# Second mixture-of-experts layer on one core: weight operands stored in order of use, their splits spread over other steps, and stores, splits and sums moved where the layers meet

## The chip, the cores and the metric

One of the eight NeuronCores of a Trainium2 chip runs the program. The metric is device time in microseconds (us) from start to end of one execution. TensorE (PE) multiplies, VectorE (DVE) and ScalarE (ACT) copy, split and add, GpSimd (POOL) adds and issues DMAs, SyncE (SP) issues DMAs. Each engine takes its instructions in the order in which they are written and waits for others through semaphores.

## What is computed

```python
# 2304 tokens: q, k, v are (4, 8, 576, 64); all is fp32 (the first layer's weights come as float64)
kv  = einsum('bhsd,bhse->bhde', k, v)
out = einsum('bhsd,bhde->bhse', q, kv)
x   = out / sqrt(mean(out*out, -1) + 1e-6) * g_norm            # -> (2304, 512)
h   = maximum(maximum(x @ w1, x @ w2), x @ w3)                 # 768 wide
y   = h @ w_out                                                # (2304, 512)
p   = probs / (probs.sum(-1) + 1e-9)                           # 4 experts
for e in range(4):                                             # the second layer
    out += p[:, e:e+1] * (maximum(y @ e_w1[e], 0) @ e_w2[e])   # 1024 wide
```

## The kernel before

Attention and most of the first layer fill the trace up to about 360 us. The change concerns the second layer and the stretch in which it takes over from the first, which is called **the turn** here.

**Tiling of the second layer.** The tokens are six blocks of 384, two to a superblock (`sb` 0, 1, 2). The hidden units of the four experts are eight halves, the **passes** (`q` 0 to 7). A pass goes over the three superblocks, forwards or backwards in turn; a pass and a superblock make a **visit** (24 of them, `gi`). Both matrix products are done by a 2x2 block scheme with seven products in place of eight (Winograd's). Each fp32 operand is split into a high part in the PE's reduced format and a low part (what is left), and high x high, low x high and high x low are summed.

A visit has two **half-visits**, `n` = 0 to 47 (`r = n % 2`), and each of these has seven **steps**, `k` = 0 to 6. In a step the PE does `product(r, k)` of the first matrix product (six matmuls of 384 columns, line 605), then ACT and DVE take the sums out of two PSUM banks (`A` and `X`) in `after_product`, then the PE does 8 to 10 matmuls of 256 columns (line 866, `AFTER`) of the second matrix product of the visit before, whose results are scaled and stored by `after_second`. So the second product lags a visit behind. The last visit's second product stands alone at the end.

**Within a step.** The bank sequence of the seven products is A X A X A A X. After product 0 ACT copies A into X (line 659, `bank<-bank`) and product 1 adds to it, so product 1 waits for the copy. After product 4 ACT takes A out as `t22` and DVE adds X to it (line 646, `fa<-bank`), and product 6, which writes X, waits for that sum. After product 6 DVE adds X to `t12` (line 682), and the next half-visit's copy into X waits for it. What becomes the second product's operands is split later, by a table of steps (`later`, `todo`).

**Weights.** While half-visits 0 to 5 of a pass run, the next pass's weights come in: `w1_load` and `w2_load` (SP queue), the block sums of the scheme (`w1_sums` line 530, `w2_sums` line 559), and the splits: a high part by ACT (lines 536 and 565), then a low part by DVE (lines 500 and 566), 0.8 to 1.2 us each. Each operand has seven 256-column pieces; the split is done in two parts, of pieces 0 to 2 and 3 to 6. The second product uses its pieces in the order `j` = 0, 1, 3, 2, 5, 4, 6, and piece `j` stands in place `j`. A table, `plan`, filled by `at(n, step, function, ...)`, says after which step each of these is written; what is due runs at the end of its step.

**Activations.** A superblock's seven split operands (`y_split(k)`: ACT line 591, DVE line 500) are made in pass 0 from `y` (loaded from DRAM buffers `y_d` by `y_load`, with sums `y_sum`, line 582), stored to DRAM (`op_store`, line 1125) and loaded again in the later passes, one after each product that has freed its place (`op_load`, line 1129). A load into a place waits for those that still read it; an ACT or DVE write into a buffer waits for a DMA that still reads it.

**The turn.** Half-visits 0 and 1 have no earlier visit; half-visit 0 does the rest of the first layer's last product between its steps (`FILL_18`), half-visit 1 nothing. `y_put` (line 439) and `rest1` (line 791) store the first layer's last two blocks of results to `y_d` straight from buffers in the tile `fa`, which half-visit 1 uses again for `t12`, `t22` and their like.

Of the kernel before, what the change touches and what calls it, by code (L numbers as in the profile page):

```python
# [21 lines left out]
def tile_attn_moe_moe2(  # L22
# [28 lines left out]
    P = 128  # L51
# [381 lines left out]
    def y_put(j, c, bank, t):  # L433

        if c % 2 and j < 4:
            nc.vector.tensor_copy(out=t, in_=bank)
        else:
            nc.scalar.activation(out=t, in_=bank, func=AF.Copy)
        nc.sync.dma_start(out=y_rows(j, c), in_=t)
# [29 lines left out]
    SPLIT = {(8, 1): (0,), (8, 2): (1,), (8, 4): (2,), (8, 6): (3,), (0, 0): (4,), (0, 2): (5,), (0, 3): (6,)}  # L469
# [62 lines left out]
    def w1_split(r, half, early=False):  # L532
        cols = slice(0, 3 * 2 * P) if half == 0 else slice(3 * 2 * P, 7 * 2 * P)
        hi, lo = w1_slot(r)
        src = w1_at(early)[half][:, 2 * P if half == 0 else 0 :]
        nc.scalar.activation(out=hi[:, cols], in_=src, func=AF.Copy)  # L536
        low(lo[:, cols], src, hi[:, cols])

# [6 lines left out]
    def w2_load(q, r):  # L545
        e, pr = q // 2, q % 2 * 2 + r
        st = w2_at(q, r).rearrange("p (n d) -> p n d", n=8)
        for a, (x, y) in enumerate(((0, 7), (2, 4))):
# [102 lines left out]
    def after_product(n, k):  # L651
# [127 lines left out]
    def rest1(sb, p, blk, c):  # L779
# [10 lines left out]
        if p == NPF - 1:  # L790
            nc.sync.dma_start(out=y_rows(2 * sb + 1, c), in_=y)
# [5 lines left out]
    YLAG = 3  # L797
# [98 lines left out]
    with tc.manual_schedule():  # L896
# [354 lines left out]
```

## Time and profile before

| | us |
|---|---|
| median of 3 runs (lowest, highest) | 1131.92 (1130.12, 1133.57) |
| the profiled execution | 1131.67 |
| its span, first to last instruction | 1129.9 |
| PE busy (share of the span) | 1078.0 (95%) |
| DVE busy | 768.4 (68%) |
| ACT busy | 591.7 (52%) |

The span leaves out what lies around the first and the last instruction, 1.8 us here. An engine is busy while an instruction of it runs; in the matmul engine's case the ends are modelled, so that what counts is its idle time and what ended it. The half-visits of the second layer start at 360.5 us (n = 0), and the last step of the last one at 1103.5 us.

### The profile page before, as it was taken

The numbers are of one execution on the slowest core, as the hardware profiler recorded it, in microseconds if no ns is written. First come the engines' busy times: TensorE is split into PE (matmuls) and PEld (weight loads), VectorE is DVE, ScalarE is ACT, GpSimd is POOL, SyncE is SP. The second block draws the span as 40 slices with busy tenths as digits, with TensorE's granted clock in tenths as the row PEclk, the third lists the DMA queues.
The fourth block names the chain that finished last, engine by engine and source line by source line (L and its number), as shares of the span: only waits on it lengthen the run. The fifth ranks groups of instructions, "written<-read, shape, count | busy, mean of one in ns | idle before, by whom it ended". The sixth has DMA issues, their size and how long they took to land.

```text
span 1129.9 us, 19220 instructions
## 1 busy us (share of the span) xinstructions
PE 1078.0 (95%) x7318; PEld 1056.9 (94%) x7318; DVE 768.4 (68%) x1434; ACT 591.7 (52%) x1257; POOL 236.1 (21%) x261
## 2 busy tenths in 40 slices
PE   7889999999999799999999999999999999999997
PEld 6789999999998699999999999999999999999997
DVE  3789985667666877765765675675576577567545
ACT  2544224434343567555565565666556566556551
POOL 1346632430101001112111212112212211121111
PEclk8999999999999899999999999999999999999998
DMA  9955555431512858359577667768858957766875
GB/s 248 293 149 170 158 177 201 137 112 65 172 44 94 304 218 288 122 224 287 96 238 235 145 183 222 192 138 223 238 102 243 269 114 225 221 158 171 226 193 113
DMA packets 110460, 209.17 MB, mean 185 GB/s; under 512 B 13856, under 2 KB 68128, under 8 KB 110368
## 3 DMA queue, kind: packets, MB, share of 16 engines
q1 hardware_dynamic: 90704, 171.44, 45.8%
q0 software_dynamic: 18960, 36.19, 18.5%
q8 instruction: 57, 0.93, 0.3%
q10 hardware_dynamic: 704, 0.33, 0.1%
q14 instruction: 35, 0.29, 0.1%
HBM read 137.93 MB, written 69.99 MB: 184 GB/s over the span
## 4 chain that ended last, share of the span: by engine, by line
PE 59%; DVE 16%; DMA 8%; issue 7%; ACT 7%; SPq 1%; POOL 1%; DVEq 0%; ACTq 0%; POOLq 0%
PE bank L605 33%; PE bank L866 21%; PE bank L772 4%; DMA w_da<-cv_a 1%; PE bank L424 1%; DMA w1s<-in_moe_w_dram 1%; DMA y_d<-fa 1%; DMA out_dram<-ob 1%; DMA out_dram<-w2s 1%; DVE wr L566 1%; DVE wl L500 1%; ACT wl L536 1%; ACT ob L847 1%; DVE rb L500 1%; DVE cv_a L233 1%
## 5 line engine op out<-in xcount | busy, mean ns | idle before, releaser
L866 PE MATMUL bank<-wr 128*128 128x256 f32 x1701 | 263.6, 283 | 5.0 <-DVE wr L566 2.8
L866 PEld LDWEIGHTS bank<-wr 128*128 128x128 f32 x1701 | 239.5, 190 | 5.8 <-DVE wr L566 3.4
L605 PE MATMUL bank<-rb,wl 128*128 128x384 f32 x1032 | 210.4, 339 | 8.3 <-ACT bank L659 8.2
L659 ACT ACTIVATE fa<-bank 128x384 f32<-128x384 f32 x192 | 94.9, 494 | 179.2 <-PE bank L605 172.2
L605 PEld LDWEIGHTS bank<-rb,wl 128*128 128x128 f32 x1032 | 175.3, 188 | 11.5 <-ACT bank L659 10.3
L605 PE MATMUL bank<-xr,wl 128*128 128x384 f32 x864 | 176.3, 339 | 6.4 <-DVE fa L646 4.6
L605 PEld LDWEIGHTS bank<-xr,wl 128*128 128x128 f32 x864 | 145.9, 189 | 8.8 <-DVE fa L646 6.4
L641 DVE TENSOR_TENSOR wr<-fa,wr 128x384 fp32r<-128x384 f32 x131 | 72.3, 552 | 47.8 <-ACT wr L634 47.6
L866 PE MATMUL bank<-wr,hr 128*128 128x256 f32 x558 | 93.0, 285 | 1.7 <-DVE wr L566 1.7
L824 POOL DMA_DIRECT2D out_dram<-w2s x48 | 48.5, 1037 | 200.1 <-DVE ob L849 152.0
L824 POOL DMA_DIRECT2D out_dram<-ob x48 | 48.0, 1038 | 173.2 <-DVE w2s L849 93.2
L866 PEld LDWEIGHTS bank<-wr,hr 128*128 128x128 f32 x558 | 82.0, 192 | 2.1 <-DVE wr L566 2.1
L634 ACT ACTIVATE wr<-fa 128x384 fp32r<-128x384 f32 x152 | 78.4, 529 | 5.2 <-DVE fa L646 2.4
L866 PE MATMUL bank<-wr,xr 128*128 128x256 f32 x405 | 68.1, 281 | 0.9 <-DVE wr L566 0.9
L748 DVE TENSOR_TENSOR fa<-bank,fa 128x384 f32<-128x384 f32 x54 | 29.9, 554 | 51.6 <-ACT fa L745 36.3
L605 PE MATMUL bank<-op,wl 128*128 128x384 f32 x288 | 59.7, 343 | 5.2 <-ACT fa L659 5.2
L847 ACT ACTIVATE w2s<-bank,p_all 128x256 f32<-128x256 f32 x104 | 49.4, 475 | 24.6 <-PE bank L866 24.6
L847 ACT ACTIVATE ob<-bank,p_all 128x256 f32<-128x256 f32 x102 | 48.4, 474 | 24.9 <-PE bank L866 24.1
L824 POOL DMA_DIRECT2D out_dram<-fa x37 | 34.2, 1053 | 128.8 <-DVE fa L849 72.0
L866 PEld LDWEIGHTS bank<-wr,xr 128*128 128x128 f32 x405 | 59.1, 188 | 1.1 <-DVE wr L566 1.1
L530 POOL TENSOR_TENSOR w1s<-w1s 128x256 f32<-128x256 f32 x40 | 35.2, 898 | 110.2 <-DMA w1s<-in_moe_w_dram 48.9
L682 DVE TENSOR_TENSOR fa<-bank,fa 128x384 f32<-128x384 f32 x48 | 26.6, 554 | 43.6 <-PE bank L605 43.5
(204 smaller groups left out, 2037.3 us busy)
## 6 DMA issues: line engine op xcount, KB each, us to landing
rb<-op_d SPq DMA_DIRECT2D x42, 768.0 KB, 5.0
xr<-op_d SPq DMA_DIRECT2D x42, 768.0 KB, 6.5
out_dram<-w2s POOLq DMA_DIRECT2D x47, 256.0 KB, 6.4
out_dram<-ob POOLq DMA_DIRECT2D x46, 256.0 KB, 6.6
op<-op_d SPq DMA_DIRECT2D x14, 768.0 KB, 8.1
stage_a<-in_moe_w_dram SPq DMA_DIRECT2D x18, 512.0 KB, 4.1
w1s<-in_moe_w_dram SPq DMA_DIRECT2D x30, 256.0 KB, 3.8
out_dram<-fa POOLq DMA_DIRECT2D x30, 256.0 KB, 6.6
```

What stands on the lines that cost most here:

```text
L500: nc.vector.tensor_tensor(out=lo, in0=src, in1=f32(hi), op=ALU.subtract)
L530: eng.tensor_tensor(out=st[o], in0=st[a], in1=st[b], op=ALU.subtract)
L605: nc.tensor.matmul(out, w[wi][:, c * P : (c + 1) * P], y[yi][:, c, :], start=(i == 0 and k in begin), stop=(i == 5), skip_group_check=k no ...
L634: nc.scalar.activation(out=ops[key][0], in_=src, func=AF.Relu if relu else AF.Copy)
L641: nc.vector.tensor_tensor(out=lo, in0=src, in1=f32(hi), op=ALU.subtract)
L659: nc.scalar.activation(out=out, in_=in_, func=func)
L682: nc.vector.tensor_tensor(out=t12, in0=x, in1=t12, op=ALU.add)
L748: nc.vector.tensor_tensor(out=mx[done] if i == 0 else t, in0=x, in1=t, op=ALU.add)
L772: nc.tensor.matmul(bank[:, :T], w[:, wi, c * P : (c + 1) * P], h[a, blk][hi], start=((blk == 1 or p == 0) and a == 0 and n == 0), stop=((b ...
L824: nc.gpsimd.dma_start(out=rows, in_=src, accum_op=ALU.add)
L847: nc.scalar.activation(out=o, in_=piece(ps, i), func=AF.Copy, scale=pe)
L866: nc.tensor.matmul(piece(ps, i), h[hi][:, i * P : (i + 1) * P], w[wi], start=fresh, stop=last, skip_group_check=True,)
```

## The change

The second product's pieces stand in the order of use (`n` in place of `j`), and `w2_load` and `w2_sums` put the blocks where that order wants them. A split is now two functions, the high part (`w1_hi`, `w2_hi`) and the low part (`w1_lo`, `w2_lo`), and the table puts the low part one step behind the high part. Loads, sums and splits of the weights have other steps. The sum `t22` is written right behind ACT's part of step 4, and not after the second product's results of that step. At the turn, the last two blocks' stores go to POOL's queue, three `op_store` of superblock 0 come two or three steps later, `w1_load` of the next pass comes at n = 1, and the sums and splits of superblocks 1 and 2 come two steps later. At the end, the last operands' steps are written between the matmuls of the last second product, no longer all ahead of it, and the stores of each block's middle tile go to ACT's queue.

```diff
-        nc.sync.dma_start(out=y_rows(j, c), in_=t)
+        (nc.gpsimd if j == 4 else nc.sync).dma_start(out=y_rows(j, c), in_=t)
...
-    SPLIT = {(8, 1): (0,), (8, 2): (1,), (8, 4): (2,), (8, 6): (3,), (0, 0): (4,), (0, 2): (5,), (0, 3): (6,)}
+    SPLIT = {(8, 1): (0,), (8, 2): (1,), (8, 4): (2,), (0, 0): (3,), (0, 1): (4,), (0, 2): (5,), (0, 3): (6,)}
...
+    def w1_hi(r, half, early=False):
+        hi, lo, src = w1_cols(r, half, early)
+        nc.scalar.activation(out=hi, in_=src, func=AF.Copy)
+
+    def w1_lo(r, half, early=False):
+        hi, lo, src = w1_cols(r, half, early)
+        low(lo, src, hi)
...
-        for a, (x, y) in enumerate(((0, 7), (2, 4))):
+        for a, (x, y) in enumerate(((0, 7), (3, 5))):
...
+    def w2_hi(q, r, half):
+        hi, lo, src = w2_cols(q, r, half)
+        nc.scalar.activation(out=hi, in_=src, func=AF.Copy)
+
+    def w2_lo(q, r, half):
+        hi, lo, src = w2_cols(q, r, half)
+        nc.vector.tensor_tensor(out=lo, in0=src, in1=f32(hi), op=ALU.subtract)
...
-            later(t0 + 4, nc.vector.tensor_tensor, out=t22, in0=x, in1=t22, op=ALU.add)
+            nc.vector.tensor_tensor(out=t22, in0=x, in1=t22, op=ALU.add)
...
-            nc.sync.dma_start(out=y_rows(2 * sb + 1, c), in_=y)
+            (nc.gpsimd if sb == 2 else nc.sync).dma_start(out=y_rows(2 * sb + 1, c), in_=y)
...
-    YLAG = 3
+    YLAG = (0, 5, 5)
...
-                nc.sync.dma_start(out=rows, in_=src)
+                (nc.scalar if i == 1 else nc.sync).dma_start(out=rows, in_=src)
...
-        for j in (0, 1, 3, 2, 5, 4, 6):
+        for n, j in enumerate((0, 1, 3, 2, 5, 4, 6)):
...
-                    w = [t[:, j * 2 * P : (j + 1) * 2 * P] for t in w2_slot(r)]
+                    w = [t[:, n * 2 * P : (n + 1) * 2 * P] for t in w2_slot(r)]
...
-            at(0, 5 + i, w2_split, 0, 0, i)
+            at(*((0, 5), (1, 2))[i], w2_hi, 0, 0, i)
+            at(*((0, 6), (1, 3))[i], w2_lo, 0, 0, i)
+            at(*((1, 6), (2, 1))[i], w2_hi, 0, 1, i)
+            at(*((1, 6), (2, 2))[i], w2_lo, 0, 1, i)
...
-            at(0, (0, 1, 2, 3, 5, 5, 5)[k], op_store, 0, k)
...
+                at(2 * sb - 1, (4 + i, (1, 3, 5, 6)[i])[sb - 1], y_sum, nc.vector, i)
+        for k in range(7):
+            at(0, (0, 1, 2, 3, 7, 8, 8)[k], op_store, 0, k)
+            for sb in range(1, NSB):
+                at(2 * sb - 1, k + YLAG[sb], y_split, k)
+                at(2 * sb, k + 1, op_store, sb, k)
...
-            at(n - 2, 0, w1_load, e, pr)
-            at(n - 1, 5, w1_load, e, pr + 1)
+            at(n - 5, 2, w1_load, e, pr)
+            at(n - 1, 4, w1_load, e, pr + 1)
+            at(n, 1, w1_sums, nc.vector)
...
-                at(n - 2, 5 + i, w1_sums, nc.vector, False, which)
-                at(n, 2 + i, w1_sums, nc.vector, False, which)
-                at(n - 1, 1 + 2 * i, w1_split, 0, i)
-                at(n, 4 + i, w1_split, 1, i)
+                at(n - 2 if q == 1 else n - 4, 3 + 2 * i, w1_sums, nc.vector, False, which)
+                at(n - 1, 2 * i, w1_hi, 0, i)
+                at(n - 1, 1 + 2 * i, w1_lo, 0, i)
+                at(n, 2 + 2 * i, w1_hi, 1, i)
+                at(n, 3 + 2 * i, w1_lo, 1, i)
                 for r in range(2):
-                    at(n - 1 + r, 4 + i, w2_sums, q, r, which)
-                    at(n + 1 + i, (0, 3)[r], w2_split, q, r, i)
+                    if q == 1:
+                        at(n - 1 + 2 * r, (5, 6, 0, 1)[2 * r + i], w2_sums, q, r, which)
+                    else:
+                        at(*((n - 3, 5), (n - 2, 1), (n - 2, 3), (n - 2, 5))[2 * r + i], w2_sums, q, r, which)
+                    k = (2, 4)[r] if i == 0 else (0, 2)[r]
+                    at(n + 1 + i, k, w2_hi, q, r, i)
+                    at(n + 1 + i, k + 1, w2_lo, q, r, i)
             for r in range(2):
-                at(n - 2 + r, 6, w2_load, q, r)
+                at(*((n - 2, 5) if q == 1 else (n - 4, 4)), w2_load, q, r)
...
-        for ended in second(gi - 1, *visits[gi - 1]):
+        for n, ended in enumerate(second(gi - 1, *visits[gi - 1])):
             if ended:
                 after_second(gi - 1, *visits[gi - 1], *ended)
+            if n % 9 == 8:
+                for step in todo.pop(t + 3 + n // 9, ()):
+                    step()
```

In the plan's loop over passes, `n` is 6q, the first half-visit of pass `q`. Lines of the changed kernel are 12 higher for the same statement in most of this stretch.

Place 1, DVE, steps 3 to 5 of half-visit 11 (the last before a pass). The bank is X; `w2s`, `ob` and `fa` with `p_all` are the second product's results, `wl<-w1s` is a low part of the first product's weights. Before:

```order
L649 SCALAR_TENSOR_TENSOR fa<-fa 128x384
L500 TENSOR_TENSOR wl<-w1s,wl 128x1024
L849 SCALAR_TENSOR_TENSOR w2s<-bank_66,p_all,w2s 128x256
L849 SCALAR_TENSOR_TENSOR ob<-bank_66,p_all,ob 128x256
L849 SCALAR_TENSOR_TENSOR fa<-bank_67,p_all,fa 128x256
L646 TENSOR_TENSOR fa<-fa 128x384
L646 TENSOR_TENSOR fa<-bank_72,fa 128x384
L559 TENSOR_TENSOR fa<-fa 128x256 x2
```

With the change:

```order
L661 SCALAR_TENSOR_TENSOR fa<-fa 128x384
L500 TENSOR_TENSOR wl<-w1s,wl 128x1024
L683 TENSOR_TENSOR fa<-bank_72,fa 128x384
L861 SCALAR_TENSOR_TENSOR w2s<-bank_66,p_all,w2s 128x256
L861 SCALAR_TENSOR_TENSOR ob<-bank_66,p_all,ob 128x256
L861 SCALAR_TENSOR_TENSOR fa<-bank_67,p_all,fa 128x256
L658 TENSOR_TENSOR fa<-fa 128x384
```

The sum that reads X (line 646, now 683) moved from behind the three results and another sum to right behind the low part; the weights' sums of line 559 are gone from here.

Place 2, DVE, steps 4 to 6 of half-visit 12 (the first of a pass), where line 682 reads X ahead of the next half-visit's copy. Before:

```order
L646 TENSOR_TENSOR fa<-bank_72,fa 128x384
L500 TENSOR_TENSOR wl<-w1s,wl 128x768
L559 TENSOR_TENSOR fa<-fa 128x256 x2
L641 TENSOR_TENSOR xr<-fa,xr 128x384
L500 TENSOR_TENSOR wl<-w1s,wl 128x1024
L559 TENSOR_TENSOR fa<-fa 128x256 x2
L682 TENSOR_TENSOR fa<-bank_72,fa 128x384
```

With the change:

```order
L500 TENSOR_TENSOR wl<-w1s,wl 128x768
L683 TENSOR_TENSOR fa<-bank_72,fa 128x384
L658 TENSOR_TENSOR fa<-fa 128x384
L653 TENSOR_TENSOR xr<-fa,xr 128x384
L500 TENSOR_TENSOR wl<-w1s,wl 128x1024
L694 TENSOR_TENSOR fa<-bank_72,fa 128x384
```

Four sums of line 559 and one low part went from between the two sums that read X; the low part that stays has its high part a step earlier.

Place 3, SP at the turn (n = 0 step 4 to n = 2): `y_d_90` holds block 4 of `y`, `op_d_4` to `op_d_6` are stores of split operands, `ob<-in_moe_w_dram` is `w2_load(0, 1)`. Before:

```order
L571 DMA fa<-y_d_88 128x1536
L571 DMA fa<-y_d_89 128x1536
L439 DMA y_d_90<-fa 128x384
L1125 DMA op_d_4_96<-xr 128x1536
L1125 DMA op_d_5_97<-op_1098 128x1536
L1125 DMA op_d_6_98<-xr 128x1536
L439 DMA y_d_90<-fa 128x384
L550 DMA ob<-in_moe_w_dram 128x2x256 x2
```

With the change:

```order
L583 DMA fa<-y_d_88 128x1536
L583 DMA fa<-y_d_89 128x1536
L557 DMA ob<-in_moe_w_dram 128x2x256 x2
L1137 DMA op_d_4_96<-xr 128x1536
L1137 DMA op_d_5_97<-op_1098 128x1536
L1137 DMA op_d_6_98<-xr 128x1536
L525 DMA w1s<-in_moe_w_dram 128x4x128 x2
```

The stores of `y_d_90` left the queue, the weights' load stands ahead of the three large stores, and the next pass's `w1_load` behind them. On POOL, whose queue had nothing there, the stores stand now between its last sums and the first stores of the output:

```order
L530 TENSOR_TENSOR w1s<-w1s 128x256 x4
L803 DMA y_d_91<-fa 128x384 x2
L803 DMA y_d_91<-ob 128x384 x2
L439 DMA y_d_90<-fa 128x384 x4
L838 DMA out_dram<-w2s 128x512
```

All eight stores of blocks 4 and 5 moved to POOL.

## Rows read from the trace of the kernel before

**Rows 1.** The page's head.

```profile
span 1129.9 us, 19220 instructions
```

**Rows 2.** PE's waits: who waited for whom, total us, times, longest us.

```profile
PE bank L605 <- ACT bank L659: 8.2, 9, 1.5
PE bank L866 <- DVE wr L566: 7.2, 8, 1.1
PE bank L605 <- ACT fa L659: 6.9, 3, 4.8
...
PE bank L605 <- DVE fa L646: 4.6, 8, 1.1
...
PE bank L605 <- ACT fa L745: 0.7, 2, 0.4
```

**Rows 3.** Stretches n = 13, 14, 15, 17: length, busy times, PE clock, DMA share, GB/s.

```profile
567.24:583.14 15.90, 15.14 (x108) 14.94 (x106) 13.17 (x26) 8.31 (x20) 2.65 (x3) 1.00 0.72 244
583.14:599.24 16.10, 15.23 (x107) 15.03 (x106) 8.90 (x16) 11.18 (x25) 3.46 (x4) 1.00 0.83 200
599.24:614.13 14.89, 14.89 (x108) 14.89 (x107) 8.89 (x20) 6.67 (x16) 2.61 (x3) 1.00 0.82 272
629.04:644.68 15.64, 15.13 (x108) 14.93 (x106) 13.24 (x29) 8.46 (x18) 2.61 (x3) 1.00 0.37 88
```

**Rows 4.** DVE in order of time, n = 11: start, us, what.

```profile
546.88 1.22 DVE L500 TENSOR_TENSOR wl<-w1s,wl 128x1024 fp32r<-128x1024 f32 x1
...
549.66 0.55 DVE L646 TENSOR_TENSOR fa<-bank,fa 128x384 f32<-128x384 f32 x1
```

**Rows 5.** DVE, then ACT, around the start of n = 13.

```profile
567.41 1.23 DVE L500 TENSOR_TENSOR wl<-w1s,wl 128x1024 fp32r<-128x1024 f32 x1 [1.39 <-ACT wl L536]
...
569.87 0.47 ACT L659 ACTIVATE bank<-bank 128x384 f32<-128x384 f32 x1 [2.08 <-DVE fa L682]
```

**Rows 6.** ACT, then DVE, n = 14 steps 3 and 4.

```profile
592.26 1.07 ACT L565 ACTIVATE wr<-fa 128x1024 fp32r<-128x1024 f32 x1
...
593.36 1.23 DVE L566 TENSOR_TENSOR wr<-fa,wr 128x1024 fp32r<-128x1024 f32 x1 [2.63 <-ACT wr L565]
```

**Rows 7.** Stretches n = 0 to 3, the turn; columns are PE, PEld, DVE, ACT, POOL.

```profile
360.47:378.16 17.69, 16.20 (x92) 15.66 (x91) 13.73 (x23) 10.83 (x19) 0.00 (x0) 1.00 0.71 269
378.16:396.44 18.28, 10.39 (x46) 9.17 (x46) 14.77 (x25) 9.28 (x18) 0.00 (x0) 0.81 0.95 346
396.44:413.23 16.79, 15.37 (x108) 14.96 (x106) 13.29 (x22) 13.01 (x27) 0.00 (x0) 1.00 0.79 281
413.23:429.47 16.24, 15.12 (x108) 14.91 (x107) 14.09 (x26) 9.08 (x19) 1.88 (x3) 1.00 0.43 141
```

**Rows 8.** ACT in n = 1; the chain's piece that ends there (start, us, what).

```profile
391.63 0.49 ACT L659 ACTIVATE fa<-bank 128x384 f32<-128x384 f32 x1 [4.93 <-DMA y_d<-fa]
...
380.29 11.24 DMA y_d<-fa
```

**Rows 9.** The end: PE, then DVE, then SP's queue.

```profile
1108.29 0.88 PE L866 MATMUL bank<-wr,xr 128*128 128x256 f32 x6
...
1111.98 1.03 PE L866 MATMUL bank<-wr 128*128 128x256 f32 x6 [2.10 <-ACT bank L837]
1112.81 1.49 PE L866 MATMUL bank<-wr,hr 128*128 128x256 f32 x6
...
1123.81 1.27 DVE L849 SCALAR_TENSOR_TENSOR fa<-bank,p_all,fa 128x256 f32<-128x256 f32 x3 [0.89 <-PE bank L866]
...
1122.16 4.38 SPq L822 DMA_DIRECT2D out_dram<-fa  x7
```

**Rows 10.** DMA issues, whole trace: count, KB each, median us from issue to landing.

```profile
xr<-op_d SPq DMA_DIRECT2D x42, 768.0 KB, 6.5
...
out_dram<-fa POOLq DMA_DIRECT2D x30, 256.0 KB, 6.6
...
y_d<-fa SPq DMA_DIRECT2D x20, 192.0 KB, 2.0
```

More of the change, by code (lines that the diff above doesn't have):

```diff
@@ L530, in w1_sums, with w1_cols, w1_split @@
             eng.tensor_tensor(out=st[o], in0=st[a], in1=st[b], op=ALU.subtract)
-    def w1_split(r, half, early=False):
+    def w1_cols(r, half, early):
         cols = slice(0, 3 * 2 * P) if half == 0 else slice(3 * 2 * P, 7 * 2 * P)
         hi, lo = w1_slot(r)
-        src = w1_at(early)[half][:, 2 * P if half == 0 else 0 :]
-        nc.scalar.activation(out=hi[:, cols], in_=src, func=AF.Copy)
-        low(lo[:, cols], src, hi[:, cols])
+        return hi[:, cols], lo[:, cols], w1_at(early)[half][:, 2 * P if half == 0 else 0 :]
+    def w1_hi(r, half, early=False):
[4 more added lines that the diff above has]
+        low(lo, src, hi)
+    def w1_split(r, half, early=False):
+        w1_hi(r, half, early)
+        w1_lo(r, half, early)
     def w2_at(q, r):
@@ L556, in w2_sums, with w2_cols @@
         st = [t[:, n * 2 * P : (n + 1) * 2 * P] for n in range(8)]
-        sums = ((1, 7, 0, ALU.subtract), (3, 1, 4, ALU.subtract), (5, 4, 7, ALU.subtract), (6, 2, 3, ALU.add))
+        sums = ((1, 7, 0, ALU.subtract), (2, 1, 5, ALU.subtract), (4, 5, 7, ALU.subtract), (6, 3, 2, ALU.add))
         for o, a, b, op in [sums[x] for x in which]:
             nc.vector.tensor_tensor(out=st[o], in0=st[a], in1=st[b], op=op)
-    def w2_split(q, r, half):
+    def w2_cols(q, r, half):
         cols = slice(0, 3 * 2 * P) if half == 0 else slice(3 * 2 * P, 7 * 2 * P)
         hi, lo = w2_slot(r)
-        src = w2_at(q, r)[:, cols]
-        nc.scalar.activation(out=hi[:, cols], in_=src, func=AF.Copy)
-        nc.vector.tensor_tensor(out=lo[:, cols], in0=src, in1=f32(hi[:, cols]), op=ALU.subtract)
+        return hi[:, cols], lo[:, cols], w2_at(q, r)[:, cols]
+    def w2_hi(q, r, half):
[4 more added lines that the diff above has]
+        nc.vector.tensor_tensor(out=lo, in0=src, in1=f32(hi), op=ALU.subtract)
     def y_load(sb, src=None):
@@ L1137, in tile_attn_moe_moe2 @@
         at(1, 5, w2_sums, 0, 1)
-        at(1, 6, w2_split, 0, 1, 0)
-        at(2, 2, w2_split, 0, 1, 1)
-        for k in range(7):
-            at(0, (0, 1, 2, 3, 5, 5, 5)[k], op_store, 0, k)
-            for sb in range(1, NSB):
-                at(2 * sb - 1, k + YLAG, y_split, k)
-                at(2 * sb, k, op_store, sb, k)
         for sb in range(1, NSB):
             for i in range(4):
-                at(2 * sb - 1, i, y_sum, nc.vector, i)
+                at(2 * sb - 1, (4 + i, (1, 3, 5, 6)[i])[sb - 1], y_sum, nc.vector, i)
[4 more added lines that the diff above has]
+                at(2 * sb, k + 1, op_store, sb, k)
         at(0, 4, y_load, 1)
@@ L1210, in tile_attn_moe_moe2 @@
         assert not any(rest)
-        for t in sorted(todo):
-            for step in todo[t]:
+        gi += 1
+        t = 14 * gi
+        for i in range(t, t + 3):
+            for step in todo.pop(i, ()):
                 step()
-        gi += 1
-        for ended in second(gi - 1, *visits[gi - 1]):
+        for n, ended in enumerate(second(gi - 1, *visits[gi - 1])):
             if ended:
                 after_second(gi - 1, *visits[gi - 1], *ended)
+            if n % 9 == 8:
+                for step in todo.pop(t + 3 + n // 9, ()):
+                    step()
+        assert not todo
         assert not plan
```

## The prediction

> **What bounds the kernel now.** I read the page's head first, then the list of the PE's waits, then the trace cut at the half-visits' first products, and last the queues of DVE, ACT and SP at the places where the PE waited. The execution's own time is 1131.67 us against a span of 1129.9 [rows 1], and the median of the three runs is 0.25 us above it, so sums are made against 1131.67 and stand for the median too. The PE is the bound: an undisturbed half-visit takes 14.89 us with the PE busy for all of it (n = 15) [rows 3], and there are 48. So only what stops the PE counts. The list of its waits names four groups in the second layer, and their counts are telling [rows 2]: nine waits for the copy into X, eight for low parts of the second weights, eight for a DVE sum that reads X, three for ACT with one of 4.8 us. Seven of each of the first, second and fourth belong to the seven passes after the first, one in n = 6q+1, one in n = 6q+2, one in n = 6q-1; the rest is the turn.
>
> **The passes.** Against 14.89 the half-visits 13, 14 and 17 have 15.90, 16.10 and 15.64 [rows 3]: 1.01 + 1.21 + 0.75 = 2.97 us a pass, the restart of the PE behind each wait included. Seven passes: 20.8 us. What becomes of each wait:
>
> In n = 6q-1 the sum that product 6 waits for starts at 549.66, behind a low part of 1.22 us that starts at 546.88 and four other DVE instructions [rows 4]. In the changed order (place 1) it stands right behind the low part, at about 548.1, 1.5 us earlier; the wait is 0.6 to 0.75 us. Gone, with some 0.8 us to spare. What is late next are the three scaled results behind it, by 0.5 us; nothing on the PE wants their banks in that step.
>
> In n = 6q+1 the copy starts at 569.87 because it waited for line 682, which stood behind a low part of 1.23 us that had itself waited 1.39 us for its high part [rows 5], and two sums. In the changed order (place 2) the high part is a step ahead, 2.1 us (14.89 / 7), and the sums are elsewhere, so that the low part ends a step before the sum. The wait of 1.0 us goes. The four `w1_sums` that now stand together at 6q, step 1, fall on a DVE that is busy for 8.9 to 13.2 of 15 us in such stretches [rows 3]; they delay nothing that reads a bank before step 4.
>
> In n = 6q+2 the second product's fourth piece waits for the last low part, which starts at 593.36, when its high part of 1.07 us ends [rows 6]. With pieces in order of use that part is wanted after 54 matmuls of the half-visit's 63, not after 36, one to two steps later, and high and low parts are written at steps 2 and 3 in place of both at 3. That moves the need by 2 us or more and the supply forward by up to 2 us against a wait of 1.2: gone, with the largest margin. The loads that moved (two DMAs of `w1_load` to 6q-5, four of `w2_load` to 6q-4) are issues on SP with several half-visits until use; their price is a rival below.
>
> I take 20.0 of the 20.8. Bounds: 14 (one wait in three comes back somewhere) and 20.8.
>
> **The turn.** Its four stretches take 17.69, 18.28, 16.79 and 16.24 us [rows 7]. In n = 0 the copy into X has the longest of its waits, 1.5 us [rows 2], with ACT's high part of operand 3 just ahead of it in the queue; that now follows the copy. DVE's part of the wait stays, so I take 0.7 of 1.5. In n = 1 the PE is busy for 10.39 of 18.28 us at a mean clock of 0.81, the half rate having come behind its longest idle time [rows 7]. ACT stood still for 4.93 us there until a store out of `fa` had landed, 11.24 us after its issue [rows 8], behind three stores of 768 KB (place 3). A store of its kind with nothing ahead takes 2.0 us, a larger, accumulating one from POOL 6.6 [rows 10]: on POOL it should take between these, 4 us taken, and free ACT at about 384 in place of 391.6.
>
> The Trainium skill's page "DMA: Bandwidth & Descriptors" (section "Issuing engines are not separate DMA queues") says that all issuers share the same 16 DMA engines, so that another issuer saves only its issue time. By that rule the store would land as late as before and n = 1 would keep most of its length; the sum by it is the first rival's. Its page "GPSIMD Engine Reference" (section "Specifications") adds that GpSimd shares its SBUF interface with VectorE when that reads two inputs, which is nearly all that DVE does here; no row before shows POOL issuing beside such a stretch at the turn.
>
> But the time is then not the PE's. DVE is busy for 14.77 + 13.29 = 28.06 of the 35.07 us of n = 1 and 2 [rows 7], and all of this is still wanted before the last product of n = 2: the second weights' sums and low parts, and the seven low parts of superblock 1, which now come two steps ahead of their product where they came four ahead. So n = 1 and 2 can't take less than 28.1; behind the last low part a step of the PE, 2 us, remains. I take 30.0, a gain of 5.1, and what is late next is a low part of `y_split` in n = 2. Bounds: 1 and 7.0. In n = 3 the wait for the sum that reads X, the longest of its kind with 1.1 us [rows 2], goes as in the passes, and two low parts leave the stretch: 1.2 of its 1.35 us over 14.89. The turn: 0.7 + 5.1 + 1.2 = 7.0; bounds 2 and 9.8.
>
> **The end.** The PE waits 2.10 us for the copies of line 837 and then runs at half rate: six matmuls in 1.49 where six took 0.88 [rows 9], two such groups, 1.2 us, 1.1 taken. The copies stood behind the high parts of operands that are wanted much later; these now come between the matmuls, the first low parts stay ahead. I leave 0.3 of the wait: 1.8 + 1.1. The last stores: DVE ends at 1123.81 + 1.27 = 1125.08, SP's seven issues run until 1126.54 [rows 9], 0.63 each; two of the last three go to ACT's queue, which is idle, so the last issue comes up to 0.9 earlier, 0.8 taken. Sum 3.7; bounds 1.5 and 4.3. **Elsewhere**, the same move of a high part in the ninth unit touches two waits of 0.7 us together [rows 2]: 0.3, bounds 0 and 0.7. Splitting functions in two and reordering pieces add no instruction.
>
> **Sum.** 20.0 + 7.0 + 3.7 + 0.3 = 31.0; 1131.67 - 31.0 = 1100.7 us.
>
> **Rivals.** (1) *The turn keeps its length.* The store from POOL lands late, or the low part of operand 0 or 1 for n = 2 comes late enough to stop the PE again and drop its clock. For it: DVE has only 7.0 us idle there [rows 7]. Against: the three large stores no longer stand ahead. The turn then gives 2: 1105.7, or 1104 to 1107.
>
> (2) *A wait comes back in every pass.* With DVE busy 13.24 of 15.64 us in n = 17 [rows 3] something that I hold harmless may stop the PE, a sum, an ACT copy behind a 1.07 us high part. One of three: 1 us x 7, so 1107.7; 1105 to 1111.
>
> (3) *Reloads come late.* `w1_load` now stands in n = 6q+1 between the third and fourth reload of an operand, `w2_load` (1 MB) just ahead of the reloads of 6q+3, where DMA is busy 0.82 of the time [rows 3]. A reload lands 6.5 us after issue in the median [rows 10] and is wanted 14.9 after it. 512 KB at the 244 GB/s of n = 13 are 2.1 us, 1 MB at the 200 of n = 14 is 5.2 us, less than the 8.4 us to spare. If the last reloads, which queue longest, are late by 1 to 2 us a pass: 1107 to 1115.
>
> (4) *Slower.* The same collision, worse: with products that wait for a reload at both places of a pass the change loses from 31.0 / 7 = 4.4 us a pass on, that is, when reloads land over 19 us after issue. At 6 us a pass the time is 1143. Nothing in the rows is near that.
>
> (5) *The change doesn't do what it says.* If the low parts a step behind still waited for ACT, nothing but the end and the turn would move: 1121. The order of place 2 speaks against it.
>
> **How the numbers follow.** The forecast, 1097 to 1104, has 0.58; rival 1 0.13; 2 and 3 0.11 each; 5 0.02; 4 0.02; within 0.3% of before, that is 3.4 us, about what a measurement of this kernel can tell from no change, 0.01; better than 1097 0.02. All but the fourth and "no change" are faster by more than 0.3%: 0.97. The bounds of the terms add up to 17.5 and 35.6 us, 1114 and 1096. Eight in ten needs the forecast, rivals 1 and 2 and the near half of 3: 1095 to 1112.
>
> **What would show it.** Half-visits 13, 14 and 17 at 14.9 us; no wait of the PE for lines 659, 646 and 566's successors beyond the turn; n = 1 and 2 together at 30 us with DVE nearly without idle time and the PE waiting for low parts of line 500; ACT's wait for `y_d<-fa` at most 2 us; the PE's wait before the last second product's third piece under 0.5 us. Wrong would be: products of n = 6q+2 or 6q+4 that wait for `op_d`, or n = 1 as long as before.

## The result, and the profile after

The changed kernel takes 1104.67 us (median of 4 runs, 1102.58 to 1105.40) against 1131.64 (median of 4, one more than in the table ahead), 27.0 us less, a ratio of 0.9758 (95% interval 0.9737 to 0.9778). The forecast was 1100.7 us with a range of 1095 to 1112: sign and range were right, the time 4 us too low, just outside the 1097 to 1104 that had most of the chances and inside the first rival's 1104 to 1107. The profiled execution is the fastest of the four, 1102.58, span 1100.8.

The PE's waits after (who waited for whom, total us, times, longest us):

```profile
PE bank L617 <- DVE rb L500: 2.3, 1, 2.3
...
PE bank L617 <- ACT bank L671: 1.5, 2, 0.8
...
PE bank L617 <- DVE xr L500: 1.1, 1, 1.1
...
PE bank L617 <- ACT fa L671: 0.6, 1, 0.6
...
PE bank L878 <- DVE wr L579: 0.4, 1, 0.4
```

Of the groups of [rows 2], the nine waits for the copy into X have become two, the eight for low parts of the second weights one, and the eight for the sum that reads X are gone. What is left of them lies at the turn, where waits for low parts of the activations (`rb`, `xr`) are new. The half-visits n = 13, 14 and 17, and everything from n = 5 to the last step of the last half-visit (columns as in [rows 3]: PE, PEld, DVE, ACT, POOL busy, clock, DMA):

```profile
558.74:573.60 14.86, 14.86 (x108) 14.86 (x106) 10.61 (x22) 8.20 (x18) 2.63 (x3) 1.00 0.86 299
573.60:588.51 14.91, 14.91 (x108) 14.91 (x106) 10.35 (x20) 11.30 (x25) 3.46 (x4) 1.00 1.07 280
618.33:633.19 14.86, 14.86 (x107) 14.86 (x106) 10.87 (x22) 8.19 (x18) 2.61 (x3) 1.00 0.24 53
439.60:1077.94 638.34, 638.34 (x4504) 638.34 (x4502) 428.37 (x854) 390.58 (x868) 118.26 (x142) 1.00 0.73 200
```

Where three half-visits of a pass were long, all are now 14.9, and in these 638 us the PE is busy without a gap. The turn, n = 0 to 4, which answers to [rows 7]:

```profile
359.09:375.89 16.80, 16.05 (x92) 15.73 (x91) 13.02 (x21) 10.20 (x19) 4.03 (x7) 1.00 0.97 360
375.89:386.34 10.45, 8.74 (x46) 7.34 (x45) 9.60 (x19) 7.96 (x17) 0.55 (x1) 1.00 0.87 324
386.34:408.71 22.37, 18.07 (x105) 16.36 (x106) 18.88 (x30) 15.06 (x29) 0.00 (x0) 0.92 0.71 253
408.71:423.56 14.85, 14.85 (x107) 14.85 (x106) 11.81 (x23) 7.44 (x17) 1.62 (x3) 1.00 0.52 189
423.56:439.60 16.04, 15.99 (x108) 14.76 (x106) 14.25 (x26) 13.69 (x29) 2.22 (x4) 1.00 0.97 352
```

n = 1 is short at last, but n = 2 has grown from 16.79 to 22.37: the sum of both fell by 2.25, not by 5.1. And n = 4, which the prediction had not named, grew; before, it and the end were these two stretches:

```profile
429.47:444.45 14.98, 14.98 (x107) 14.91 (x106) 11.37 (x22) 12.34 (x27) 2.20 (x4) 1.00 1.03 397
...
1103.45:1129.90 26.45, 18.93 (x142) 18.52 (x140) 13.77 (x30) 4.80 (x12) 3.60 (x5) 0.87 0.58 119
```

The end after, from the same place:

```profile
1077.94:1100.80 22.86, 17.34 (x142) 17.08 (x140) 13.56 (x31) 4.87 (x12) 4.21 (x5) 0.94 0.68 139
```

So the 29.1 us between the two profiled executions divide as follows:

| stretch | forecast | measured |
|---|---|---|
| up to the start of n = 0 (first layer) | -0.3 | -1.38 |
| n = 0 | -0.7 | -0.89 |
| n = 1 and 2 | -5.1 | -2.25 |
| n = 3 | -1.2 | -1.39 |
| n = 4 | 0 | +1.06 |
| n = 5 to the last step of n = 47 | -20.0 | -20.66 |
| the end | -3.7 | -3.59 |

The first line is luck for the most part. In the twelve traces with the changed first layer, this one and eleven of the kernels below, n = 0 starts between 359.09 and 361.64, around the 360.47 of before; nothing is credited to the change there. (The two waits that the prediction's 0.3 stands on, 0.7 us together, became one of 0.5.) Of the 31.0 us forecast the other lines hold 27.7, and the turn (3.47 for 7.0) is nearly all of the difference.

How n = 2 stalls: PE, then DVE, then ACT (start, us, what, idle before and what ended it), and last the stretch of 392 to 394 us, with the granted clock behind POOL's column:

```profile
389.62 0.62 PE L617 MATMUL bank<-rb,wl 128*128 128x384 f32 x2 [2.30 <-DVE rb L500]
...
385.81 1.55 DVE L566 TENSOR_TENSOR ob<-ob 128x256 f32<-128x256 f32 x4
...
388.61 0.95 DVE L500 TENSOR_TENSOR rb<-fa,rb 128x768 fp32r<-128x768 f32 x1
...
398.54 0.96 DVE L500 TENSOR_TENSOR xr<-fa,xr 128x768 fp32r<-128x768 f32 x1 [2.17 <-ACT xr L603]
...
405.28 0.96 DVE L500 TENSOR_TENSOR xr<-fa,xr 128x768 fp32r<-128x768 f32 x1
...
396.72 1.05 ACT L575 ACTIVATE wr<-ob 128x1024 fp32r<-128x1024 f32 x1
397.67 0.83 ACT L603 ACTIVATE xr<-fa 128x768 fp32r<-128x768 f32 x1
...
392.00:394.00 2.00, 2.00 (x8) 1.99 (x8) 2.00 (x4) 0.84 (x1) 0.00 (x0) 0.50 0.26 92
```

The low part of operand 0 stands on DVE behind the second weights' four sums, the PE stops for 2.30 us and then runs at half rate (a granted clock of 0.50, the lower of its two levels, 1.2 GHz) for some 3 us. ACT gets its copies late from the late PE, and so it makes the next high part late; DVE, which had been busy without a gap since 380.5, waits 2.17 us for that. The last low part of superblock 1 is the one of 405.28.

### The profile page after: what moved, and what is told of

Its sections match the earlier page's. It is cut to its first block, busy times and chain, and to the rows that moved or that the text cites. A ratio compares the mean times of both kernels' runs of the same rounds, so it can differ in the third digit from the quotient of the medians.

```text
span 1100.8 us, 19219 instructions
## 1 busy us (share of the span) xinstructions
PE 1070.6 (97%) x7318; PEld 1051.7 (96%) x7318; DVE 768.7 (70%) x1434; ACT 593.9 (54%) x1257; POOL 238.8 (22%) x269
## 4 chain that ended last, share of the span: by engine, by line
PE 63%; DVE 0%; issue 0%; DVEq 0%
PE bank L878 32%; PE bank L617 30%; DVE wr L579 0%; DVE xr L500 0%; DVE fa L861 0%; DVE hr L653 0%; DVE hr L651 0%; DVEq L1271 0%
## 5 line engine op out<-in xcount | busy, mean ns | idle before, releaser
L760 DVE TENSOR_TENSOR fa<-bank,fa 128x384 f32<-128x384 f32 x54 | 29.9, 554 | 51.8 <-ACT fa L757 36.5
L694 DVE TENSOR_TENSOR fa<-bank,fa 128x384 f32<-128x384 f32 x48 | 26.7, 557 | 49.2 <-PE bank L617 49.2
L683 DVE TENSOR_TENSOR fa<-bank,fa 128x384 f32<-128x384 f32 x48 | 26.7, 557 | 48.0 <-ACT fa L671 47.2
```

Of the source, the lines that this page charges most:

```text
L683: nc.vector.tensor_tensor(out=t22, in0=x, in1=t22, op=ALU.add)
L694: nc.vector.tensor_tensor(out=t12, in0=x, in1=t12, op=ALU.add)
L760: nc.vector.tensor_tensor(out=mx[done] if i == 0 else t, in0=x, in1=t, op=ALU.add)
```

## The experiments

Besides the times, which tell 1 us from nothing only just, each trace is read stretch by stretch. The stretches repeat well: n = 3 and 4 together took 30.89 to 30.91 in all traces whose code there is that of the changed kernel. The sum of n = 1 and 2 is less sharp: it came out at 32.82 in the changed kernel and at 32.27, 32.28, 32.30, 32.66 and 32.84 in five kernels below that leave these two as they are. A difference within 0.6 us says nothing there.

### The turn: when superblock 1 is split

```diff
-    YLAG = (0, 5, 5)
+    YLAG = (0, 3, 5)
-                at(2 * sb - 1, (4 + i, (1, 3, 5, 6)[i])[sb - 1], y_sum, nc.vector, i)
+                at(2 * sb - 1, (i, (1, 3, 5, 6)[i])[sb - 1], y_sum, nc.vector, i)
```

> The changed kernel with superblock 1's sums and splits at their old steps (sums at steps 0 to 3 of n = 1, splits from step 3 on), all else as changed. Theory A, the low parts of operands 0 and 1 are late in n = 2 because they are written two steps later: the PE's wait of 2.30 us at the start of n = 2 and the half rate behind it go, n = 1 and 2 together fall from 32.8 to 28.5 to 30 us and the time from 1104.7 to about 1101. Theory B, DVE's work before that point is the limit whatever its order: what comes earlier there pushes the sums of n = 1's own products back, n = 1 grows by what n = 2 loses, and the time stays within 1 us of 1104.7.

1105.04 us, ratio 0.9761 (0.9746 to 0.9776). n = 1 and 2:

```profile
376.98:390.70 13.72, 10.10 (x46) 8.61 (x45) 13.65 (x23) 9.53 (x19) 0.55 (x1) 0.86 0.93 336
390.70:409.91 19.21, 16.69 (x106) 16.29 (x106) 14.66 (x26) 13.25 (x27) 0.00 (x0) 0.92 0.91 335
```

No wait for operand 0 is left, but DVE is busy for 13.65 of the 13.72 us of n = 1, and the PE waits there for the sums of its own products instead; 32.93 together. B: the stall is moved, not removed. (The change had moved these splits by two steps, but these sums by four.)

### The turn: the stores back on SP

```diff
-        (nc.gpsimd if j == 4 else nc.sync).dma_start(out=y_rows(j, c), in_=t)
+        nc.sync.dma_start(out=y_rows(j, c), in_=t)
-            (nc.gpsimd if sb == 2 else nc.sync).dma_start(out=y_rows(2 * sb + 1, c), in_=y)
+            nc.sync.dma_start(out=y_rows(2 * sb + 1, c), in_=y)
```

> The changed kernel with the eight stores of blocks 4 and 5 of y back on SP's queue; the three large op_store stay where the change put them. Theory A, POOL's queue is what freed ACT in n = 1: ACT waits for a store out of fa again, by 3 us or more, n = 1 goes from 10.5 back to 14 to 18 us and the time to 1107 to 1111. Theory B, the three large stores ahead of it were the cause and their move alone freed ACT: n = 1 stays below 12 us and the time within 1 us of 1104.7.

1106.68 us, ratio 0.9772 (0.9755 to 0.9789). n = 1 and 2, ACT in n = 1, and SP's issue of the two loads of superblock 1's `y`, 768 KB each:

```profile
377.26:391.45 14.19, 10.25 (x45) 9.00 (x45) 10.89 (x22) 8.17 (x17) 0.00 (x0) 0.88 1.02 369
391.45:412.11 20.66, 16.67 (x108) 14.73 (x106) 17.71 (x27) 14.82 (x29) 0.00 (x0) 1.00 0.68 251
...
384.85 0.49 ACT L671 ACTIVATE fa<-bank 128x384 f32<-128x384 f32 x1 [2.58 <-DMA y_d<-fa]
...
375.98 1.25 SPq L583 DMA_DIRECT2D fa<-y_d  x2
```

The same issues in the changed kernel, and ACT's first wait for such a store in the kernel before (the second is that of [rows 8]):

```profile
364.54 5.84 SPq L583 DMA_DIRECT2D fa<-y_d  x2
```

```profile
385.47 0.49 ACT L659 ACTIVATE fa<-bank 128x384 f32<-128x384 f32 x1 [1.50 <-DMA y_d<-fa]
```

Between the two: n = 1 is back at 14.19, ACT waits 2.58 us (1.50 + 4.93 before the change), and n = 1 and 2 take 34.85, 2.0 more than in the changed kernel and as much as before (35.07). POOL's queue thus made nearly all of the gain in n = 1 and 2. All else that the change does here, the later places of the three large stores among it, took 3.85 us off ACT's wait and 0.2 off the two stretches, which is inside their scatter.

The two traces differ in what SP can issue. On SP the two loads stand behind stores that wait for their data, and the last two stores stand behind the loads. With the stores on POOL the loads are issued 5.5 to 11.3 us into n = 0, not 15.5 to 16.8, and are all but over when the last stores come. Beside large transfers a store lands no sooner from POOL: the first seven take 4.4 to 7.4 us there, the last, with the loads all but over, 2.8; from SP the first four take 1.8 to 2.0, with nothing large ahead, the other four 4.2 to 7.4. By these traces the gain is that the loads no longer wait for the stores, and not a quicker transfer from POOL. No run changes the order on SP alone, which would test it.

### The turn: the PE kept busy in front of the stall

```diff
-                    for half, w in ((0, 4 * P), (1, 2 * P)):
+                    for half, w in ((0, 4 * P),) * 11 + ((1, 2 * P),):
```

> The changed kernel with ten more matmuls of 512 columns at the start of n = 2, into the bank that the two matmuls there already write and that is written anew afterwards; some 2.3 us of PE work in front of a wait of 2.30 us. Theory A, the half rate behind that wait is a cost of its own: with the PE kept busy the granted clock stays at 1.00 in n = 2 (0.92 in the changed kernel), the busy time there, which is 3.2 us over that of a full-rate half-visit, falls by 2 us or more beside the added work, and n = 2 takes 19.5 to 21 in place of 22.4, the time about 1102.5. Theory B, DVE's low parts are the limit in all of n = 2: the waits for them grow by what the faster PE gains, n = 2 stays above 21.8 us and the time within 0.7 us of 1104.7.

1103.79 us, ratio 0.9749 (0.9736 to 0.9762). The added matmuls fall into the first of the two stretches:

```profile
378.48:390.73 12.25, 10.88 (x55) 9.34 (x55) 11.40 (x22) 9.73 (x19) 0.55 (x1) 1.00 0.87 312
390.73:410.78 20.05, 16.65 (x108) 14.71 (x106) 17.11 (x27) 13.27 (x27) 0.00 (x0) 1.00 0.72 264
```

The clock stays at 1.00 and n = 2 at 20.05, as A has it, but the sum is 32.30, inside the spread of the unchanged turn. The half rate is gone and the two stretches are not shorter: B. The slow PE only filled time in which it would have waited.

### The turn: less work on DVE, and work in order of its due time

First the four sums of the second weights, done on POOL:

```diff
-        at(1, 5, w2_sums, 0, 1)
+        at(1, 2, w2_sums, 0, 1, (0, 1, 2, 3), nc.gpsimd)
```

> The changed kernel with one thing more: the four sums of w2_sums(0, 1), 1.55 us of DVE in n = 1, are done by POOL, which is idle there, three steps earlier. Theory B (DVE's load sets the length of n = 1 and 2): 1.3 to 1.6 us come off the 32.8 of n = 1 and 2 together. Rival (DVE waits for others there and its load doesn't matter, 4.3 us idle): the two stretches stay at 32.4 to 33. POOL's sums may also slow DVE's own instructions beside them; then DVE's busy time in n = 1 and 2 falls by less than 1.55 from 28.48.

1104.74 us, ratio 0.9765 (0.9744 to 0.9787); n = 1 and 2 take 32.98. DVE's busy time there is 29.24, more than the 28.48 with the sums. DVE, then POOL, in n = 1:

```profile
381.83 0.56 DVE L653 TENSOR_TENSOR wr<-fa,wr 128x384 fp32r<-128x384 f32 x1 [0.78 <-ACT wr L646]
382.31 1.10 DVE L651 SCALAR_TENSOR_TENSOR wr<-fa,wr 128x384 fp32r<-128x384 f32 x1
383.33 1.09 DVE L653 TENSOR_TENSOR wr<-fa,wr 128x384 fp32r<-128x384 f32 x1
384.34 1.08 DVE L661 SCALAR_TENSOR_TENSOR fa<-fa 128x384 f32<-128x384 f32 x1
...
382.12 3.90 POOL L566 TENSOR_TENSOR ob<-ob 128x256 f32<-128x256 f32 x4 [2.84 <-DMA ob<-in_moe_w_dram]
```

While POOL adds, DVE's instructions of 0.55 us take 1.09. The 1.55 us taken away came back as 2.3. So this one does not tell the two theories apart.

Then the order, with the sums on DVE:

```diff
-    YLAG = (0, 5, 5)
+    YLAG = (0, 4, 4)
...
+                at(*(((1, 4), (2, 0), (1, 5), (2, 2)), ((3, 2), (4, 0), (3, 5), (4, 2)))[sb - 1][i], y_sum, nc.vector, i)
...
-            at(*((0, 5), (1, 2))[i], w2_hi, 0, 0, i)
-            at(*((0, 6), (1, 3))[i], w2_lo, 0, 0, i)
+            at(*((0, 5), (2, 0))[i], w2_hi, 0, 0, i)
+            at(*((0, 6), (2, 1))[i], w2_lo, 0, 0, i)
...
-        at(1, 5, w2_sums, 0, 1)
+        at(1, 5, w2_sums, 0, 1, (0, 1))
+        at(2, 0, w2_sums, 0, 1, (2, 3))
...
-                at(n - 2 if q == 1 else n - 4, 3 + 2 * i, w1_sums, nc.vector, False, which)
+                at(*((n - 3, i) if q == 1 else (n - 4, 3 + 2 * i)), w1_sums, nc.vector, False, which)
```

> The changed kernel with the work of n = 1 to 4 in order of its due times. For n = 2 the splits of superblock 1 begin one step earlier, with each sum just ahead of the split that needs it; the second parts of the second weights' splits, wanted after 54 of the second product's matmuls, and the sums for them go behind the low part of operand 0. For n = 4 the splits of superblock 2 begin one step earlier, the first of the sums of the next pass's first weights, 1.6 us of DVE in n = 4, go to the start of n = 3, where DVE is idle. Theory B: n = 1 and 2 together are bound by 28.5 us of DVE; with the first low part no longer late the PE's wait of 2.30 us and the half rate go, and n = 1 and 2 fall from 32.8 to 30 to 31.5. Rival: order doesn't matter there (as little as in the kernel with earlier sums and splits, 32.9), 32.3 or more. n = 3 and 4 together fall from 30.9 to 29.8 to 30.2 if n = 4 lacks only DVE time. The time is 1101 to 1102.5, or above 1104 by the rival.

1103.27 us, ratio 0.9750 (0.9734 to 0.9766), the lowest median, but not to be told from the changed kernel by it. n = 1 to 4:

```profile
376.81:386.76 9.95, 8.58 (x46) 7.47 (x46) 8.36 (x16) 7.25 (x16) 0.55 (x1) 1.00 0.87 331
386.76:408.99 22.23, 17.15 (x108) 16.54 (x106) 20.06 (x33) 15.85 (x30) 0.00 (x0) 0.92 0.78 270
408.99:423.83 14.84, 14.84 (x107) 14.84 (x106) 12.32 (x26) 8.17 (x18) 1.62 (x3) 1.00 0.44 174
423.83:439.49 15.66, 15.27 (x108) 14.99 (x106) 13.78 (x23) 13.07 (x28) 2.22 (x4) 1.00 1.01 355
```

n = 1 and 2 still take 32.18, with another wait in the old one's place (2.75 us for the low part of the second weights). n = 3 and 4 give 0.39 us, real but small.

Both edits together, with all four sums on POOL:

> Both: work in order of its due times, and w2_sums(0, 1) on POOL. Theory B: DVE's busy time in n = 1 and 2 is 27.0, and the two stretches take 28.5 to 30.5 in place of 32.8, the time 1099.5 to 1101.5. Rival: neither matters, 32.3 or more.

1104.19 us, ratio 0.9761 (0.9742 to 0.9780). n = 1 and 2 take 34.09, 1.3 more than in the changed kernel; DVE's busy time did not fall (28.61). A loss where a gain was expected, with POOL's sums beside DVE again.

### n = 4: superblock 2 split earlier

```diff
-    YLAG = (0, 5, 5)
+    YLAG = (0, 5, 3)
-                at(2 * sb - 1, (4 + i, (1, 3, 5, 6)[i])[sb - 1], y_sum, nc.vector, i)
+                at(2 * sb - 1, (4 + i, 1 + i)[sb - 1], y_sum, nc.vector, i)
```

> The changed kernel with superblock 2's sums at steps 1 to 4 and its splits from step 3 of n = 3 on, two steps earlier. Theory A, n = 4 takes 16.04 in place of 14.89 because each low part there ends just as its product wants it: n = 4 falls to 14.9 to 15.1, n = 3, where DVE is idle for 3 us, stays at 14.85, and the time falls by 1.0 to 1103.7. Theory B, the work only goes where it hurts as much: n = 3 grows by 0.7 us or more, as before the change (16.24), and n = 3 and 4 together stay at 30.9 or rise.

1104.37 us, ratio 0.9751 (0.9736 to 0.9765). n = 3 stays at 14.85; n = 4 takes 15.77, only 0.27 less. What stopped the PE in n = 4, in the changed kernel (PE's weight loads, for low parts) and here:

```profile
PEld bank L617 <- DVE xr L500: 0.7, 2, 0.4
PEld bank L617 <- DVE rb L500: 0.5, 2, 0.3
```

```profile
PE bank L617 <- ACT bank L671: 0.6, 1, 0.6
```

The low parts were what was late (A), but with them early the copy into X is late instead: it starts at 428.06, when ACT is done with three results and high parts (427.96) and DVE with the sum of line 694 (427.97).

### The passes: one line of the change alone

```diff
-            later(t0 + 4, nc.vector.tensor_tensor, out=t22, in0=x, in1=t22, op=ALU.add)
+            nc.vector.tensor_tensor(out=t22, in0=x, in1=t22, op=ALU.add)
```

in the kernel before.

> The kernel before with one line of the change: the sum t22 is written right behind ACT's part. Step of the prediction: the wait of the PE for that sum (eight waits, 4.6 us) goes in n = 6q-1, which falls from 15.64 to 14.9 in each of the seven passes, and in n = 3; time -5 to -6.5 us, to about 1126. Rival: the three scaled results behind it, 0.5 us later, or the copies on ACT that wait for them stop the PE in their place: within 1 us of the kernel before.

1126.53 us, ratio 0.9960 (0.9945 to 0.9975): 4.4 us faster. Its n = 3, 4 and 17:

```profile
413.34:428.19 14.85, 14.85 (x107) 14.85 (x106) 12.71 (x23) 8.03 (x17) 1.36 (x3) 1.00 0.35 120
428.19:444.11 15.92, 15.14 (x108) 14.94 (x107) 12.76 (x24) 13.25 (x29) 2.72 (x5) 1.00 1.03 390
627.17:642.04 14.87, 14.87 (x107) 14.87 (x106) 11.60 (x25) 8.46 (x18) 1.98 (x3) 1.00 0.32 80
```

The wait in n = 6q-1 is gone by this line alone, 0.77 us in n = 17, and n = 13 and 14 keep theirs (15.88 and 16.08). It also shows where the gain in n = 3 went: n = 3 fell by 1.39 and n = 4 rose by 0.94, with the splits of superblock 2 still at their old steps.

### The passes: each of the other parts undone

Pieces back in place `j` (`w2_load`, `w2_sums` and the second product's slices), steps as changed:

> The changed kernel with the second product's pieces in the old places (place j, w2_load and w2_sums accordingly), so that the second part of the split is wanted by the third piece in the order of use, after 36 matmuls; all steps as changed. Theory A, the order of use was needed for the third kind of wait (eight waits, 7.2 us before): the PE waits for low parts of the second weights again in n = 6q+2, 0.3 to 1.2 us in each pass, time +2 to +8. Theory B, the low parts written a step or two earlier suffice alone: no wait in the passes, time within 1 us of 1104.7.

1103.39 us, ratio 0.9759 (0.9743 to 0.9776). High and low part of the first weights in one step:

```diff
-                at(n - 1, 1 + 2 * i, w1_lo, 0, i)
+                at(n - 1, 2 * i, w1_lo, 0, i)
-                at(n, 3 + 2 * i, w1_lo, 1, i)
+                at(n, 2 + 2 * i, w1_lo, 1, i)
```

> The changed kernel with each low part of the first product's weights in the step of its high part again, DVE's other sums where the change has them. Theory A, the one step between them is what took the wait for the copy into X away (seven waits of 1.0 us and their restarts): DVE stands 1.4 us before the low part, the sum of line 694 is late, n = 6q+1 goes from 14.86 back to 15.4 to 15.9, time +4 to +7. Theory B, the weights' sums that left that stretch were the cause, and DVE can wait without harm: n = 6q+1 stays below 15.0, time within 1 us of 1104.7.

1104.19 us, ratio 0.9764 (0.9750 to 0.9779). The sums of both weights (`w1_sums` alike, in passes 2 to 7), and the splits of the second weights, at the steps of before:

```diff
-                        at(*((n - 3, 5), (n - 2, 1), (n - 2, 3), (n - 2, 5))[2 * r + i], w2_sums, q, r, which)
-                    k = (2, 4)[r] if i == 0 else (0, 2)[r]
+                        at(n - 1 + r, 4 + i, w2_sums, q, r, which)
+                    k = (0, 3)[r]
                     at(n + 1 + i, k, w2_hi, q, r, i)
-                    at(n + 1 + i, k + 1, w2_lo, q, r, i)
+                    at(n + 1 + i, k, w2_lo, q, r, i)
```

> The changed kernel with two things of the passes undone, which act in different half-visits. First, the weights' sums of passes 2 to 7 are at their old steps (four of the second and two of the first weights between the sums that read X in n = 6q), with each low part still a step behind its high part. If these sums alone made the wait for the copy into X, n = 6q+1 goes from 14.86 back to 15.4 to 15.9 in six passes, +3 to +6 us; if the DVE's wait for the high part and the sums are only together too much, n = 6q+1 stays below 15.0. Second, the splits of the second weights are at their old steps (high and low part in one step), with the pieces in order of use. If the order of use alone suffices, as the prediction had it, n = 6q+2 stays at 14.91; if the earlier steps did it, n = 6q+2 goes back to 15.5 to 16.1 in seven passes, +4 to +8. The time is 1104.7 plus what comes back.

1103.87 us, ratio 0.9757 (0.9734 to 0.9780). n = 14 with the old places, n = 13 with the low part in one step with the high part, n = 13 and 14 with the sums and the second splits back:

```profile
574.30:589.21 14.91, 14.91 (x107) 14.91 (x106) 10.34 (x20) 11.31 (x25) 3.46 (x4) 1.00 1.08 289
```

```profile
558.73:573.60 14.87, 14.87 (x108) 14.87 (x106) 10.62 (x22) 8.20 (x18) 2.64 (x3) 1.00 0.83 280
```

```profile
560.59:575.46 14.87, 14.87 (x108) 14.87 (x107) 10.79 (x22) 7.97 (x18) 2.64 (x3) 1.00 0.84 290
575.46:590.36 14.90, 14.90 (x107) 14.90 (x106) 8.90 (x16) 11.18 (x25) 3.46 (x4) 1.00 1.07 276
```

Nothing comes back in any of the three, in any pass. Each wait of [rows 5] and [rows 6] has been removed twice over: the order of use alone suffices for the second weights, and so do the earlier steps alone; for the copy into X the sums may stay, and, in another kernel, the low part may follow its high part in one step (DVE then waits 0.34 us for it, not 1.39, since the high parts are a step earlier too). No run leaves out both cures of a wait in the changed kernel; the one-line kernel, which has neither, keeps both waits.

### The end

```diff
-        for i in range(t, t + 3):
+        for i in sorted(todo):
```

> The changed kernel with the last operands' steps written ahead of the last second product, as before the change; the stores stay on two queues. Step of the prediction: the wait of 2.1 us for ACT's copies and the half rate behind it come back at the end: +2.9, the stretch from the last half-visit's start to the end of the span grows from 35.7 to 38.6 us. Rival: high parts in the new order don't stand in front of the copies: under +0.5. What then is left of the 3.6 us that the end gave is the stores' two queues, about 0.7.

1106.11 us, ratio 0.9785 (0.9769 to 0.9801). From the same place to the end, and the wait:

```profile
1079.66:1105.00 25.34, 17.41 (x142) 17.01 (x140) 13.74 (x31) 4.87 (x12) 4.22 (x5) 0.93 0.64 125
...
1088.19 0.98 PE L878 MATMUL bank<-wr 128*128 128x256 f32 x6 [2.10 <-ACT bank L849]
1089.01 0.88 PE L878 MATMUL bank<-wr,hr 128*128 128x256 f32 x6
...
1098.50 1.27 DVE L861 SCALAR_TENSOR_TENSOR fa<-bank,p_all,fa 128x256 f32<-128x256 f32 x3 [0.89 <-PE bank L878]
```

The wait comes back to the hundredth (2.10). The half rate does not: the second six matmuls behind it take 0.88, where before the change they took 1.49 [rows 9], and the clock is 1.00 there. DVE's last instruction and ACT's last issues in the changed kernel:

```profile
1094.60 1.27 DVE L861 SCALAR_TENSOR_TENSOR fa<-bank,p_all,fa 128x256 f32<-128x256 f32 x3 [0.89 <-PE bank L878]
...
1093.35 3.34 ACTq L834 DMA_DIRECT2D out_dram<-fa  x3
```

The end of DVE's last instruction divides the stretch into what the PE sets and what the last stores set. Up to it the stretch takes 21.63 us before the change (1125.08 - 1103.45), 20.11 with the wait but without the half rate (1099.77 - 1079.66), and 17.93 in the changed kernel (1095.87 - 1077.94). So the wait with its restart is worth 2.18 us and the half rate 1.52. Behind it come 4.82, 5.23 and 4.93 us. In the twelve traces with the stores on two queues this last piece takes 4.8 to 5.3 us, in the two with SP alone 4.7 and 4.8: the second queue is worth nothing. The last issue does come 0.64 us sooner after DVE's end, but its store then takes 3.33 us to land in place of 2.55.

## Why the prediction was right, and where it wasn't

**The passes** were right in size (20.66 for 20.0; 638 us without a stop) and in naming one wait for each of three half-visits. The mechanism was right for the sum `t22`, by itself worth 4.4 us. For the other two the causes that it named suffice but are not needed: the step-apart low part and the order of use can each be undone without loss, as the rest of the change has enough in hand. Rivals 2, 3 and 5 did not happen: no product waits for `op_d`.

**n = 1 and 2** is the term that was mis-sized, 2.25 for 5.1. ACT's wait in n = 1 went as said, by POOL's queue; the failed step is "behind the last low part a step of the PE, 2 us, remains. I take 30.0". It took DVE for busy without a gap up to its last low part. Its busy time is 28.48, near the 28.06 reckoned with, but it is idle for 4.34 us: 0.78 and 2.17 for ACT's high parts, and, behind its last low part, 1.26 for the PE. That low part ends 30.35 us after the start of n = 1 (406.24 - 375.89) and not 28.06, and behind it come 2.47 us and not 2. Rival 1's second half happened, and the time is in that rival's range: the low part of operand 0 is 2.30 us late and the clock falls. But neither the lateness nor the clock sets the length: with operand 0 early it is 32.93, without half rate 32.30, in another order 32.18. What held is that order and clock move the stall about, while DVE's load, 28.3 to 28.5 in these, and some 4 us of mutual waiting stay. That less load would shorten it has not been shown, since the one way tried, POOL, slowed DVE.

**n = 3** was right (1.39 for 1.2), but 1.06 of it was given back in n = 4, where the prediction looked for nothing. The one-line kernel shows the same exchange without the new steps. Read from the waits, and not tested by itself: with n = 3 shorter, the same ACT and DVE work meets an earlier n = 4, and is late with low parts or, with these earlier, with the copy into X.

**The end** was right in sum (3.59 for 3.7) by errors that cancel: the wait with its restart was worth 2.2, not 1.8, the half rate 1.5, not 1.1, the second queue of stores nothing, not 0.8. That the sum came out is luck.

**The rule of the Trainium skill** weighed there. "DMA: Bandwidth & Descriptors" (section "Issuing engines are not separate DMA queues") says that another issuer saves only issue time; by that, n = 1 would have kept its length. Here the second issuer was worth 2.0 us. For the transfers the trace agrees: beside the loads a store from POOL took as long as one from SP. What the rule leaves out is that a load behind a waiting store waits with it, here the first of the two for 10 us. At the end nothing large waits behind the stores, and the second issuer was worth nothing.

## What to carry to other kernels

Removing a stall from one stretch is worth what the next stretch can take up: sum the stretches as far as the gain could be given back, here n = 1 with 2 and n = 3 with 4. A busy time is a floor, not a length, when two engines feed each other in order; put an allowance for mutual waits on top of it (here some 4 us in 33). An issuing engine takes its DMAs in order, so look for large loads behind a store that still waits for its data. When several edits serve one wait, undo each alone before crediting any; here either of two could be left out.

## What the hardware showed unexpectedly

POOL's additions and DVE's instructions beside them take turns: four 128x256 additions on POOL took 3.90 us, 0.98 each, and DVE's 128x384 instructions started 1.0 us apart in place of 0.47. The Trainium skill's page "SBUF — State Buffer" (section "SBUF: two separate sides") describes the port that these two engines share as locked for a whole instruction; the trace agrees.

The clock after a wait is not settled by the wait's length. After the same 2.10 us at the end the PE fell to the lower clock in the kernel before and in the one-line kernel (the second six matmuls behind the wait in 1.49 and 1.42 us), and stayed at 1.00 in the kernel with the operands' steps ahead again (0.88). What decides it has not been found out here.
